# Segment sums of x moved from TensorE to GpSimd beside a VectorE-heavy scan stage

## The chip, the cores and the metric

One core of a Trainium2 chip (the jobs ran on different chips, each with runs of the kernel before beside it). The metric is device time in microseconds (us) of one execution. Engine names in profile lines: PE is TensorE (PEld its weight load), DVE is VectorE, ACT is ScalarE, POOL is GpSimd, SP is SyncE, whose queue issues most DMAs. SBUF and PSUM are the memories that the kernel's tiles lie in; the matmuls here write PSUM tiles (psP, psU, psR). A profile's span is about 1.7 us shorter than the time of the same execution (1262.2 and 1263.91 for the changed kernel). Times in the text count from the start of the profile's span.

## The reference, cut to what matters

Two independent branches, concatenated: a diagonal state space model (A) and a segment-recurrent attention with 8 memory slots (B).

```python
# A: per step t   h = Lam_bar * h + B_bar @ x[t];  y = 2 Re(C h) + x * D       (2048 steps, 1024 states)
# B: per segment of 32 tokens: h = [mem, xs]; q, k, v = h Wq, h Wk, h Wv
#    p = softmax(mask(q k^T * scale)); o = (p v) Wo; mem = o[:, :8]; out = o[:, 8:]
```

B's recurrence through `mem` is serial. The kernel avoids it by a guess: it estimates each segment's new memory from the mean of the segment's inputs (`xbar`), runs all segments at once, and at the end compares the guess with what came out. If the guess is off by more than a tolerance, a slow serial branch computes everything again. The change is about how the 64 segment sums behind `xbar` are formed.

## The kernel before

The stage that matters lasts from about 36 to 340 us. It interleaves two streams: 32 scan blocks of A (`stage1`, called block 0 to 31 below) and the value projection of B (`v_x`, four PSUM tiles each). One scan block, cut:

```python
for i in range(2):                       # TensorE: 16 matmuls into psU (2 buffers)
    for c in range(KC):
        PE.matmul(u[:, i, :], bt[:, i, c, :], xT[:, c, cols], ...)
V.tensor_tensor(pr, u (broadcast), tables, mult)        # a_pr: one input PSUM, one SBUF
V.tensor_tensor(w, w, pr[:, :, 1, :], add)              # both inputs SBUF
for j in range(2):
    V.tensor_tensor_scan(w[:, j], rr, w[:, j], carry)   # two scans, SBUF
    S.activation(g[:, j], w[:, j], Copy)                # a_g: ScalarE
# GpSimd: five tiny instructions (a_tt, a_nx) make the carry of the next block
V.tensor_tensor(n, g (broadcast), r3, mult)             # a_n: SBUF, SBUF
V.tensor_tensor(h, n[:, :, 0], n[:, :, 1], add)         # a_h: SBUF, SBUF
SP.dma_start(hs[tb][:, pc], h)
```

The segment sums, cut. `ind` is a 128 x 4 indicator of the four segments in a tile of 128 tokens:

```python
p = k.ps("R")
for t in range(16):                          # two tiles a block, blocks 3 to 10, before stage1
    for c in range(8):
        PE.matmul(p[:, o:o + 4], xr[:, c * 128:(c + 1) * 128], ind, start=True, stop=True)
    load(t + 4); yield
# VectorE: xbar = p / 40, plus mem0 in segment 0
```

The next reader of `xbar` (the matmuls called `og`) comes at 170 us.

## Time and profile before

| | before |
|---|---|
| time, median | 1247.91 us (1247.30 to 1248.12, 4 runs) |
| span of the profile | 1246.5 us |
| PE waits between 36 and 172 us | none |
| VectorE busy between 36 and 172 us | 116.55 of 136 us |

The page of the kernel before: the span, busy time of each engine, and the chain of work that ended last by engine.

```profile
span 1246.5 us, 20192 instructions
PE 1238.4 (99%) x8342; PEld 662.2 (53%) x8342; DVE 668.1 (54%) x1246; ACT 263.4 (21%) x631; POOL 276.5 (22%) x412
...
PE 97%; DMA 2%; ACT 1%; issue 0%; POOL 0%; DVE 0%; SPq 0%; ACTq 0%
```

The view by stretches, before. Columns: stretch, its length, then busy us and instruction count of PE, PEld, DVE, ACT and POOL, the granted TensorE clock, DMA share and GB/s.

```profile
36.00:172.00 136.00, 136.00 (x773) 63.87 (x772) 116.55 (x106) 55.75 (x99) 31.67 (x50) 1.00 0.62 168
```

PE is never idle here (136.00 of 136 us) and its granted clock is 1.00, so each microsecond taken from it should be gained. VectorE is at 86%.

One group of the sums on PE, before, in the timeline: start, length, engine, line, operation, output from input, shapes, count.

```profile
67.27 0.54 PE L64 MATMUL psR<-ind,b_xr 128*128 128x4 bf16 x16
67.67 0.59 PE L64 MATMUL psU<-a_xT,a_bt 128*128 128x512 bf16 x2
```

The 16 matmuls delay the next group by 0.40 us, 25 ns each. Four columns are only about a hundredth of a 512-column matmul, which takes 216 ns here (the 16 of one half into psU: 3.45 us), yet each of the small ones costs 25 ns, over a tenth of it. Eight such groups are 3.2 us of the critical path.

VectorE in block 5, before. The bracket at a line's end is the idle time before it and what ended it.

```profile
92.84 2.29 DVE L267 TENSOR_TENSOR a_pr<-psU,a_tabf 128x2048 f32<-128x2048 f32 x1 [1.18 <-PE psU L64]
95.17 1.23 DVE L270 TENSOR_TENSOR a_pr<-a_pr 128x1024 f32<-128x1024 f32 x1
96.50 2.46 DVE L275 TENSOR_TENSOR_SCAN a_pr<-a_rr,a_nx,a_pr 128x512 f32<-128x512 f32 x2
99.66 1.23 DVE L286 TENSOR_TENSOR a_n<-a_g,a_tabh 128x2048 bf16<-128x2048 bf16 x1 [0.69 <-ACT a_g L276]
100.92 0.69 DVE L287 TENSOR_TENSOR a_h<-a_n 128x1024 bf16<-128x1024 bf16 x1
103.60 2.29 DVE L267 TENSOR_TENSOR a_pr<-psU,a_tabf 128x2048 f32<-128x2048 f32 x1 [1.99 <-PE psU L64]
```

After `a_h` VectorE waits 1.99 us for PE: here it keeps up. In the blocks that also compute tables it does not, and idles less.

### The profile page before, as it was taken

What the parts mean: (1) busy time and instruction counts of PE and PEld (TensorE: products, weight loads), DVE (VectorE), ACT (ScalarE), POOL (GpSimd) and SP (SyncE); (2) the same over time, 40 slices, a digit from 0 to 9 for tenths busy, and PEclk for the clock granted to TensorE, in tenths of its full rate; (3) what the DMA queues carried; (4) which work ended last, traced back from release to release, by engine and by line L of the source; (5) the groups of instructions that cost most, each with busy time, mean ns of one, the idle gap of its engine ahead of it and who ended that gap; (6) DMA issues with size and microseconds to landing.
All of it is one profiled execution on the core that took longest, in us unless ns stands there. A gap on an engine that the chain in (4) does not pass through costs nothing.

```text
span 1246.5 us, 20192 instructions
## 1 busy us (share of the span) xinstructions
PE 1238.4 (99%) x8342; PEld 662.2 (53%) x8342; DVE 668.1 (54%) x1246; ACT 263.4 (21%) x631; POOL 276.5 (22%) x412
## 2 busy tenths in 40 slices
PE   9999999999999999999999999999999999999998
PEld 4444444444455555656666656555665554446444
DVE  4688899998711124666666666666666641001000
ACT  5344444443310000211111111111211110000000
POOL 4111331212322321322222222222222220000000
PEclk9999999999999999999999999999999999999999
DMA  9975444554898734665454544545473279407000
GB/s 236 267 205 150 130 131 128 144 156 108 240 322 248 250 116 94 182 176 122 96 144 108 144 108 113 138 91 133 97 155 95 60 222 225 107 18 153 17 17 27
DMA packets 316023, 176.83 MB, mean 142 GB/s; under 512 B 138651, under 2 KB 301327, under 8 KB 315927
## 3 DMA queue, kind: packets, MB, share of 16 engines
q1 hardware_dynamic: 293830, 147.95, 48.4%
q10 hardware_dynamic: 21072, 24.38, 5.8%
q0 software_dynamic: 1024, 3.17, 0.7%
q8 instruction: 66, 1.08, 0.4%
q14 instruction: 31, 0.25, 0.1%
HBM read 89.14 MB, written 53.17 MB: 114 GB/s over the span
## 4 chain that ended last, share of the span: by engine, by line
PE 97%; DMA 2%; ACT 1%; issue 0%; POOL 0%; DVE 0%; SPq 0%; ACTq 0%
PE psP L64 81%; PE psU L64 9%; PE psS L64 3%; PE psO L64 2%; PE psR L64 2%; DMA wo<-in_B_Wo_dram 1%; DMA b_vx<-b_vst 1%; DMA b_xr<-in_B_x_dram 0%; ACT b_vst L89 0%; ACT L187 0%; ACT b_xe L89 0%; POOL b_m L643 0%; ACT a_fr L236 0%; ACT a_k L233 0%; ACT a_k L229 0%
## 5 line engine op out<-in xcount | busy, mean ns | idle before, releaser
L64 PE MATMUL psP<-b_xe,b_wq 128*128 128x480 bf16 (+1 forms) x1280 | 247.7, 343 | 0.0
L64 PE MATMUL psP<-b_xe,b_wk 128*128 128x480 bf16 (+1 forms) x1280 | 247.7, 343 | 0.0
L64 PE MATMUL psP<-b_wv,b_xe 128*128 128x512 bf16 (+2 forms) x1048 | 224.6, 372 | 0.3 <-ACT b_xe L89 0.2
L643 POOL TENSOR_TENSOR b_m<-b_e,maskB 99x396 bf16<-99x396 bf16 x160 | 139.6, 872 | 334.8 <-ACT b_e L640 334.8
L640 ACT ACTIVATE b_e<-psS 99x396 bf16<-99x396 f32 x176 | 88.2, 501 | 532.8 <-PE psS L64 528.5
L64 PEld LDWEIGHTS <-b_wk 128*128 128x128 bf16 x1280 | 119.4, 98 | 94.2
L64 PEld LDWEIGHTS <-b_xe 128*128 128x128 bf16 x1056 | 101.9, 98 | 119.4 <-issue 0.6
L64 PEld LDWEIGHTS <-b_wq 128*128 128x128 bf16 x1280 | 118.7, 98 | 87.7
L91 DVE CAST b_k<-psP 128x480 bf16<-128x480 f32 (+1 forms) x192 | 98.2, 533 | 100.9 <-PE psP L64 100.9
L91 DVE CAST b_q<-psP 128x480 bf16<-128x480 f32 (+1 forms) x192 | 98.2, 533 | 93.1 <-PE psP L64 91.5
L64 PEld LDWEIGHTS <-b_ol 128*128 128x128 bf16 x864 | 84.3, 98 | 94.4
L64 PE MATMUL psU<-a_xT,a_bt 128*128 128x512 bf16 x512 | 114.9, 379 | 0.0
L64 PE MATMUL psP<-t,a_hl 128*128 128x512 bf16 x512 | 113.1, 379 | 0.0
L91 DVE CAST b_ost<-psP 128x512 bf16<-128x512 f32 (+1 forms) x17 | 11.5, 676 | 183.4 <-PE psP L64 183.4
L64 PE MATMUL psP<-wo,b_ol 128*128 128x512 bf16 (+1 forms) x448 | 92.5, 364 | 0.0
L64 PE MATMUL psP<-t,b_ol 128*128 128x512 bf16 x416 | 92.2, 379 | 0.0
L280 POOL TENSOR_SCALAR a_tt<-a_pr,a_tabf 128x1 f32<-128x1 f32 x48 | 34.1, 710 | 243.5 <-DVE a_pr L275 243.5
L660 DVE TENSOR_TENSOR b_ob<-psO,b_accR 99x384 bf16<-99x384 f32 x160 | 85.9, 553 | 2.5 <-DVE b_accR L659 0.3
L89 ACT ACTIVATE b_vst<-psP 128x512 bf16<-128x512 f32 x126 | 72.1, 589 | 71.4 <-PE psP L64 60.3
L267 DVE TENSOR_TENSOR a_pr<-psU,a_tabf 128x2048 f32<-128x2048 f32 x32 | 73.0, 2283 | 14.8 <-PE psU L64 14.7
L64 PEld LDWEIGHTS <-a_bt 128*128 128x128 bf16 x512 | 49.2, 98 | 57.6
L64 PEld LDWEIGHTS <-a_hl 128*128 128x128 bf16 x512 | 49.0, 98 | 56.7
(199 smaller groups left out, 964.2 us busy)
## 6 DMA issues: line engine op xcount, KB each, us to landing
b_v<-b_vx SPq DMA_DIRECT2D x16, 1122.0 KB
b_wv<-in_B_Wv_dram SPq DMA_DIRECT2D x16, 1024.0 KB
b_on<-b_ob SPq DMA_DIRECT2D x15, 960.0 KB
b_vx<-b_vst ACTq DMA_DIRECT2D x24, 544.0 KB
a_hs<-a_h SPq DMA_DIRECT2D x32, 256.0 KB
b_wog<-in_B_Wo_dram SPq DMA_DIRECT2D x4, 2048.0 KB
b_wq<-in_B_Wq_dram SPq DMA_DIRECT2D x16, 512.0 KB
b_wk<-in_B_Wk_dram SPq DMA_DIRECT2D x16, 512.0 KB
```

Of the source, the lines that this page charges most:

```text
L64: r = f(*a, **kw)
L89: self.S.activation(out, in_, ACT.Copy)
L91: self.V.tensor_copy(out, in_)
L267: V.tensor_tensor(pr[:], u[:].unsqueeze(1).to_broadcast([128, 2, 2, TB]), view(t3, [[TB + 1, 2], [TB + 1, 2], [1, TB]]), ALU.mult)
L280: G.tensor_scalar(tt[:, j:j + 1], w[:, j, TB - 1:TB], t3[:, 1, TB:TB + 1], None, ALU.mult)
L640: k.S.activation(e[:], s[0:GW], ACT.Exp, scale=float(E) ** -0.5, accum_out=self.accE[0:GW, i:i + 1])
L643: k.G.tensor_tensor(m[0:GW, 0:4 * GW].rearrange("p (a b q) -> p a b q", a=2, b=2), e[:], mask[0:GW, :, :].unsqueeze(2).to_broadcast([GW, 2 ...
L660: V.tensor_tensor(self.ob[:, b0:b0 + n, :], o[0:GW, 0:n, 0:E], r.unsqueeze(2).to_broadcast([GW, n, E]), ALU.mult)
```

## The change

It takes the 128 small matmuls off TensorE. Rows of x are loaded so that partition p holds tokens 16p to 16p+15. GpSimd adds the 16 rows in float32, two rows a scan block, placed behind the block's carry so that the carry isn't delayed. This leaves half-segment sums, split into a high and a low bfloat16 part; 16 matmuls with a 128 x 64 indicator join the halves.

```diff
-    k.ind = c.tile([128, 4], BF16, name="ind")
-    ... four memsets
+    k.ind = c.tile([128, NSEG], BF16, name="ind")
+    ... two affine_selects: 1 where partition // 2 == segment
 def sum_x:
-        for t in range(TT):
-            for c in range(KC):
-                k.PE.matmul(p[:, o:o + 4], xr[:, c * 128:(c + 1) * 128], k.ind[:], start=True, stop=True)
-            load(t + 4)
-            yield
+        for j in range(1, 16):
+            a = xrs.pop(0)[:] if j == 1 else acc
+            G("tensor_tensor", acc, a, xrs.pop(j)[:], ALU.add)      # pinned in program order
+            load(j + 3)
+            if j == 1:
+                load(4)
+            if j % 2 == 0:
+                yield
+        G("tensor_copy", hl[:, 0, :], acc)
+        yield
+        G("tensor_tensor", hl[:, 1, :], acc, hl[:, 0, :], ALU.subtract)
         yield
+        for c in range(KC):
+            for i in range(2):
+                k.PE.matmul(p[:, c * NSEG:(c + 1) * NSEG], hl[:, i, c * 128:(c + 1) * 128], k.ind[:], start=(i == 0), stop=(i == 1))
 main loop:
-                if n >= 3:
-                    for _ in range(2):
-                        next(sx, None)
                 a.stage1(pc, q)
+                if n >= 2:
+                    next(sx, None)
```

The adds fall in blocks 2 to 9, the copy in 9, the subtract in 10, the join after the matmuls of block 11.

More of the change, by code (lines that the diff above doesn't have):

```diff
@@ L106, in consts @@
     k.S.activation(k.hpe[:], k.hpb[:], ACT.Exp)
-    k.ind = c.tile([128, 4], BF16, name="ind")
-    G.memset(k.ind[:], 0.0)
-    for j in range(4):
-        G.memset(k.ind[32 * j:32 * j + 32, j:j + 1], 1.0)
+    k.ind = c.tile([128, NSEG], BF16, name="ind")
+    G.memset(k.ind[:], 1.0)
+    for base, m in ((0, 1), (1, -1)):
+        G.affine_select(out=k.ind[:], in_=k.ind[:], compare_op=ALU.is_ge, fill=0.0, base=base,
+                        pattern=[[-2 * m, NSEG]], channel_multiplier=m)
 def masks(k):
@@ L377, in fill @@
         z = tmp.tile([32, 4 * EW], BF16, name="b_xr", bufs=4)
-        k.V.memset(z[:], 0.0)
+        k.tc.keep_in_program_order(k.V.memset(z[:], 0.0))
         for hb in range(HB):
@@ L410, in turn_x0, with sum_x, G, load @@
         k.copy("vs"[i % 2], self.xe[:, :, 128 * i:128 * i + 128], pt)
-    def sum_x(self, tmp):
+    def sum_x(self, tmp, ct):
         k = self.k
+        def G(op, *a):
+            k.tc.keep_in_program_order(getattr(k.G, op)(*a))
+        acc, hl = ct[:, 0, 0:2, :].rearrange("p c d -> p (c d)").bitcast(FP32), ct[:, 0, 2:4, :]
+        rows = self.x[0].rearrange("(p j) d -> p j d", j=16)
         xrs = {}
-        def load(t):
-            if t < TT:
-                xrs[t] = tmp.tile([128, D], BF16, name="b_xr", bufs=4)
-                k.SP.dma_start(xrs[t][:], self.x[0][t * 128:(t + 1) * 128, :])
-        for t in range(4):
-            load(t)
+        def load(j):
+            if j < 16:
+                xrs[j] = tmp.tile([128, D], BF16, name="b_xr", bufs=4)
+                k.SP.dma_start(xrs[j][:], rows[:, j, :])
+        for j in range(4):
+            load(j)
+        yield
[8 more added lines that the diff above has]
+        G("tensor_copy", hl[:, 0, :], acc)
+        yield
+        G("tensor_tensor", hl[:, 1, :], acc, hl[:, 0, :], ALU.subtract)
         yield
         p = k.ps("R")
-        for t in range(TT):
-            xr = xrs.pop(t)
-            for c in range(KC):
-                o = c * NSEG + 4 * t
-                k.PE.matmul(p[:, o:o + 4], xr[:, c * 128:(c + 1) * 128], k.ind[:], start=True, stop=True)
-            load(t + 4)
-            yield
+        for c in range(KC):
+            for i in range(2):
+                k.PE.matmul(p[:, c * NSEG:(c + 1) * NSEG], hl[:, i, c * 128:(c + 1) * 128], k.ind[:], start=(i == 0), stop=(i == 1))
         pv = p[:].rearrange("p (c s) -> p c s", c=KC)
@@ L1019, in kernel_main @@
             loads = [[(b, 2)], [(a, 1), (a, 2)], [(b, 3), (a, 3)]]
-            sx = b.sum_x(p1)
+            sx = b.sum_x(p1, a.CT)
             tabs = {0: a.tabs}
```

## The prediction

> **What bounds it now.** TensorE. The page gives PE 99% busy of a 1246.5 us span at full clock, and the chain of waits is 97% PE; the list of waits between 30 and 330 us shows no PE wait at all. So a PE microsecond taken away is gained, and a PE wait put in is lost. VectorE is second in the stage touched: by stretches it is busy 31.95 of 35 us (101 to 136) and 32.6 of 36 (136 to 172).
>
> **Removed.** 128 matmuls psR<-ind,b_xr of 4 columns. The timeline of PE shows 8 groups of 16, each delaying the next group by 0.40 us (67.27 to 67.67): 3.2 us, all on the chain.
>
> **Added on PE.** 16 matmuls with 64 columns. The og matmuls of that shape take 0.93 us for 32 (170.62 to 171.55), so about 0.47 us. Net PE gain: 2.7 us, 0.2%.
>
> **Added on GpSimd.** 15 adds, a copy and a subtract of 128x1024. The same shape (a_xd) takes 2.12 us, so about 36 us between 68 and 150 us, on an engine 20 to 28% busy there. It fits, but it is not free:
>
> 1. VectorE and GpSimd. [...] an a_nx pair normally takes 0.53 us, but 3.56 us at 163.57, while VectorE runs two-input instructions back to back. So each add waits for, or blocks, the adds, scans and a_n/a_h products. The multiply that reads PSUM (a_pr, 2.29 us) should leave room for one add per block. I expect 4 to 10 us of VectorE delay by the tenth scan block. VectorE may lag 8 to 13 us before psU holds PE up, so this alone should cost PE nothing.
>
> 2. The join. In program order, which PE keeps, the 16 matmuls stand after stage1 of block 11. With the old groups gone PE gets there at about 146.7 us. They need the subtract, which is behind the carry of block 10; that carry ends at 147.8 us before. VectorE can be 2 to 3 us earlier (PE feeds it sooner, the xbar operations move back), but the contention makes it later. Subtract done at 148 to 156 us: a new PE wait of 1 to 9 us, which nothing gives back. This is the main doubt; the next reader of xbar is only at 170 us.
>
> 3. The SP queue, in order, now waits for adds before reloading row buffers. The load of b_wv for head block 2 (issued at 69.8 us, needed at 81) slips to about 74: perhaps 0 to 2 us of PE wait. One row is also loaded twice, which costs nothing by itself.
>
> **Sum.** -2.7 us, plus about 4.5 us of waits in 2 and 3: 1250 us, range 1244.8 (no wait) to 1257. Faster by over 2%: 1%; within 2%: 97%; slower by over 2%: 2%. If the subtract is in time, it is 1245.3.
>
> **What would show it.** Right: the ind matmuls fall from 128 to 16 and about 0.5 us; the waits of PE or its weight load show some us for GpSimd (subtract) near 147 us; adds of 2.1 us alone but up to 4 us against VectorE; everything after 330 us unchanged in length. Wrong: no wait there (then -2.7 us), or PE waits for psU (VectorE fell further behind than 8 us), or for b_wv.
>
> **What would make it wrong.** Adds much slower than 2.1 us in float32; the scheduler ordering VectorE differently, as at 109 us where a_pr of block 7 overtook a_n of block 6; [...] the scans starve and the lag passes 13 us (then 1260 or more).

## More of the kernel before

`v_x` does 8 matmuls into each psP tile (3 buffers), and ScalarE copies each tile out (`b_vst<-psP`). ScalarE's queue holds these copies and the `a_g` copies in one fixed order.

## The result

The changed kernel takes 1263.91 us (median of 4 runs, 1262.34 to 1263.99); before, 1247.91. The ratio is 1.0126, 95% interval 1.0109 to 1.0144. The forecast was 1250 with 1257 as the upper end: the direction was right, the loss was 16 us instead of 2.

The page after: span, busy times, chain by engine.

```profile
span 1262.2 us, 19918 instructions
PE 1238.3 (98%) x8159; PEld 661.3 (52%) x8230; DVE 689.3 (55%) x1246; ACT 263.6 (21%) x631; POOL 316.8 (25%) x427
...
PE 90%; DVE 7%; issue 1%; POOL 1%; DMA 1%; ACT 0%; SPq 0%; ACTq 0%; DVEq 0%
```

DVE does the same 1246 instructions, yet is busy 21.2 us longer, and 7% of the chain is now on it. POOL is 40 us longer; the forecast was about 36.

The view by stretches after, same columns.

```profile
36.00:172.00 136.00, 123.14 (x550) 54.92 (x560) 122.65 (x88) 50.15 (x88) 66.09 (x62) 0.96 0.60 162
```

The list of what PE waited for between 36 and 172 us, after: total us, times, longest. A third row, 0.2 us of issue before psU, is left out.

```profile
PE psP L64 <- ACT b_vst L89: 8.8, 4, 3.2
PE psR L64 <- POOL t L419: 3.2, 1, 3.2
```

PE is idle for 136 - 123.14 = 12.9 us, and its clock is 0.96 of full, another 0.04 x 136 = 5.4 us (an estimate; the clock has two places, so about 5). Less the 2.7 us of saved matmuls that is about 15.6 us, and the spans differ by 15.7. The `og` matmuls agree: the first group starts at 170.62 us before and 186.49 after, a later one at 308.10 and 323.97, both 15.9 us late. So all of the loss has arisen by the first `og`, whose lines are, before and after:

```profile
170.62 1.10 PE L64 MATMUL psR<-b_xbar,b_wv 128*128 128x64 bf16 x32
186.49 1.10 PE L64 MATMUL psR<-b_xbar,b_wv 128*128 128x64 bf16 x32
```

Where VectorE's 21 us come from: VectorE in block 5 after, to be held against the lines of before, and below it GpSimd at the same time.

```profile
99.69 1.23 DVE L271 TENSOR_TENSOR a_pr<-a_pr 128x1024 f32<-128x1024 f32 x1
101.02 2.46 DVE L276 TENSOR_TENSOR_SCAN a_pr<-a_rr,a_nx,a_pr 128x512 f32<-128x512 f32 x2
104.17 1.23 DVE L287 TENSOR_TENSOR a_n<-a_g,a_tabh 128x2048 bf16<-128x2048 bf16 x1 [0.70 <-ACT a_g L277]
105.43 2.65 DVE L288 TENSOR_TENSOR a_h<-a_n 128x1024 bf16<-128x1024 bf16 x1
108.00 2.28 DVE L268 TENSOR_TENSOR a_pr<-psU,a_tabf 128x2048 f32<-128x2048 f32 x1
```

```profile
104.41 1.05 POOL L283 TENSOR_TENSOR a_nx<-a_nx,a_tt 128x2 f32<-128x2 f32 x1
105.41 4.66 POOL L419 TENSOR_TENSOR t<-t,b_xr 128x1024 f32<-128x1024 f32 x2
```

`a_h` takes 2.65 us instead of 0.69. The last carry instruction (1.05 us from 104.41, against 0.20 at 115.03) lasts until about the end of `a_n` at 105.40; then the first add starts at 105.41, 0.02 us before `a_h`. That add ends at 107.5 (alone in the timeline it is 2.12 us long), and `a_h` 0.55 us later. The second add runs beside the next `a_pr`, which stays at 2.28 us. The idle time before `a_pr` is gone. So "behind the carry" is a costly place for one of the two adds and, in this block, a free place for the other.

The group of `a_h` after, 60 to 170 us (before, its mean is 683 ns), and VectorE's waits for psU from 60 to 200 us, first before, then after:

```profile
L288 DVE TENSOR_TENSOR a_h<-a_n 128x1024 bf16<-128x1024 bf16 x9 | 19.7, 2190 | 0.3
```

```profile
DVE a_pr L267 <- PE psU L64: 8.5, 6, 2.0
DVE a_pr L268 <- PE psU L64: 1.9, 2, 1.6
```

By the means of the groups, `a_h` makes up about 13.6 us of VectorE's growth. The rest is on the `a_pr` adds (about 3.9), the scans (3.3) and `a_n` (1.0), where an add ran at another moment: in block 3, which has no carry to wait for, one add ran beside the `a_pr` add (3.05 us instead of 1.23) and the next beside the two scans (4.13 instead of 2.46).

How a late VectorE reaches PE: ScalarE and PE after.

```profile
105.14 0.37 ACTq L509 DMA_DIRECT2D b_vx<-b_vst  x1
112.96 0.63 ACT L277 ACTIVATE a_g<-a_pr 128x512 bf16<-128x512 f32 x1 [7.85 <-DVE a_pr L276]
114.14 0.63 ACT L277 ACTIVATE a_g<-a_pr 128x512 bf16<-128x512 f32 x1 [0.55 <-DVE a_pr L276]
114.67 1.07 ACT L89 ACTIVATE b_vst<-psP 128x512 bf16<-128x512 f32 x2
```

```profile
107.21 5.34 PE L64 MATMUL psP<-b_wv,b_xe 128*128 128x512 bf16 x23
115.30 2.86 PE L64 MATMUL psP<-b_wv,b_xe 128*128 128x512 bf16 x8 [2.75 <-ACT b_vst L89]
```

ScalarE stands 7.85 us before `a_g`, for the scan. The copies that empty psP are behind it in its queue. PE fills its three psP tiles in 5.3 us and stops. A late VectorE thus stops PE through ScalarE's order and psP, not through psU, where the forecast looked for it.

Last, the clock. Short stretches after, same columns, around that wait:

```profile
107.00:115.00 8.00, 5.50 (x25) 2.44 (x25) 7.86 (x6) 1.49 (x3) 4.91 (x6) 1.00 0.76 193
115.00:117.00 2.00, 1.70 (x6) 0.68 (x6) 2.00 (x2) 1.36 (x4) 1.97 (x2) 0.77 0.00 0
117.00:119.00 2.00, 2.00 (x6) 0.73 (x5) 2.00 (x2) 2.00 (x5) 1.92 (x2) 0.50 0.00 0
119.00:121.00 2.00, 2.00 (x10) 0.83 (x8) 2.00 (x1) 0.85 (x2) 1.92 (x2) 0.88 0.00 0
```

After the wait the clock is 0.50 for a while, and 8 matmuls take 2.86 us instead of 1.89 (as at 127.56 us, after a wait of 1.78). It is so after the waits of 3.2 us at 129 and 160 us too: 0.53 and 0.50 in the stretches 133 to 135 and 164 to 166. A wait of 2.75 us was enough here, but in run 4 a wait of the same length was not followed by it (8 matmuls in 1.89 us); what decides it was not shown.

### The profile page after: what moved, and what is told of

Its sections match the earlier page's. It is cut to its first block, busy times and chain, and to the rows that moved or that the text cites. A ratio compares the mean times of both kernels' runs of the same rounds, so it can differ in the third digit from the quotient of the medians.

```text
span 1262.2 us, 19918 instructions
## 1 busy us (share of the span) xinstructions
PE 1238.3 (98%) x8159; PEld 661.3 (52%) x8230; DVE 689.3 (55%) x1246; ACT 263.6 (21%) x631; POOL 316.8 (25%) x427
## 3 DMA queue, kind: packets, MB, share of 16 engines
q0 software_dynamic: 1024, 3.17, 0.7%
## 4 chain that ended last, share of the span: by engine, by line
PE 90%; DVE 7%; issue 1%; POOL 1%; DMA 1%; ACT 0%; SPq 0%; ACTq 0%; DVEq 0%
PE psP L64 77%; PE psU L64 7%; PE psS L64 3%; PE psO L64 2%; DVE a_pr L276 2%; DVE a_pr L268 2%; PE psR L64 1%; DVE a_pr L271 1%; DVE a_h L288 1%; DVE a_n L287 1%; DMA b_wv<-in_B_Wv_dram 1%; ACT a_g L277 0%; POOL b_m L658 0%; POOL t L419 0%; SPq L64 0%
```

## The experiments

Theory: GpSimd's adds and VectorE's instructions with two SBUF inputs exclude each other (in block 5, `a_h` takes 2.65 us instead of 0.69 beside an add); VectorE falls behind, and with it ScalarE and PE. Rivals: the row loads or the join cause the loss; GpSimd is merely busy and the carry is late.

All outputs are right.

### 1. The adds alone: before_adds

```diff
 # kernel before, sums on TensorE kept
+        G("memset", xa, 1.0)                            # dead data
+        for j in range(1, 16):
+            G("tensor_tensor", acc, xa if j == 1 else acc, xa, ALU.add)
+            if j % 2 == 0: yield                        # two a block, after stage1, as in the change
+        ... tensor_copy, subtract
```

> The kernel before, whole, with the same 17 GpSimd instructions of 128x1024 added at the same places, on dead data, with no load, no join and no other change. Theory (the GpSimd adds and VectorE's two-input instructions exclude each other, so VectorE falls behind, ScalarE's queue with it, and TensorE waits for psP): VectorE busy 15 to 25 us more than before, TensorE waits of 6 to 15 us for psP between 80 and 180 us, time 1256 to 1266. Rival (the row loads behind the adds in the SP queue, or the join, make the loss): no change, 1248 to 1250.

1263.40 us against 1247.95, ratio 1.0121 (1.0104 to 1.0138). The loss is there with no load, no layout and no join changed. The line of busy times on its page:

```profile
PE 1240.2 (98%) x8270; PEld 663.7 (53%) x8342; DVE 689.0 (55%) x1246; ACT 262.9 (21%) x631; POOL 316.6 (25%) x430
```

Its list of PE's waits, 36 to 172 us:

```profile
PE psP L64 <- ACT b_vst L89: 10.6, 4, 4.9
```

### 2. The same occupancy without reading: before_writes

```diff
-            G("tensor_tensor", acc, xa if j == 1 else acc, xa, ALU.add)
+            G("iota", t, pattern=[[1, 2048]], ...)      # writes SBUF, reads nothing; 17 times
```

> As before_adds, but the 17 GpSimd instructions only write (an iota of 2048 integers, some 2 us each by the 0.56 us of one of 513) and read nothing of SBUF. Theory (the shared read is what excludes): VectorE busy within 3 us of before, no TensorE wait, 1247 to 1250. Rival (GpSimd being occupied delays the carry, whatever it does): as slow as before_adds.

1248.24 against 1247.95, ratio 1.0000 (0.9983 to 1.0017). The 17 instructions took 1.83 us each, 31 us in all (the 17 of run 1: 40), and VectorE's `a_h` kept its 683 ns. In the view of groups, those writes (count, busy us, mean ns), then `a_h`:

```profile
L449 POOL IOTA t<- 128x2048 int32 x17 | 31.2, 1834 | 0.7
...
L287 DVE TENSOR_TENSOR a_h<-a_n 128x1024 bf16<-128x1024 bf16 x11 | 7.5, 683 | 0.2
```

So neither GpSimd's occupancy nor a late carry makes the loss (1248.24 us); the instructions of run 1, which read SBUF, do: beside them the mean of `a_h` (60 to 170 us) was 1957 ns, beside the writes 683.

### 3. VectorE's time alone: before_dve

```diff
+            V.tensor_tensor(acc, xa if j == 1 else acc, xa, ALU.add)   # 17 on VectorE itself, pinned, after a_h
```

> The kernel before, with nothing new on GpSimd but one memset; instead VectorE itself does 17 adds of 128x1024 on dead data, two a block after a_h (1.2 us each by the a_pr add of the same size: 21 us, what VectorE got longer by in the changed kernel). Theory (the loss is VectorE's time and what hangs on it): 1258 to 1266, with TensorE waiting for psP behind ScalarE. Rival (the loss comes from GpSimd being late with the carry): 1248 to 1252.

1256.98 against 1247.38, ratio 1.0075 (1.0061 to 1.0090): below the range of the expectation. VectorE was busy 685.9 us, 17.8 more than before, though the 17 adds took 1.22 us each, 20.7 in all: records that follow each other closely overlap a little (two adds end at 106.88 us, the next `a_pr` starts at 106.80), and overlap counts once. That this is the whole difference was not checked. PE waited 6.4 us for psP behind ScalarE, and its clock in the stretch was 0.97. So loading VectorE alone, with GpSimd left alone, brings the same waits and more than half of the loss. The missing 3 us alone need not explain the rest of the gap to run 1; that the adds' place within a block matters as well is likely, but was not separated.

### 4. The join a block later: after_late_join

```diff
         yield
+        yield
         p = k.ps("R")
```

> The changed kernel with the 16 joining matmuls one scan block later (after stage 1 of block 12). Theory: the 3.2 us wait for the subtract goes, and the slow matmuls after it (about 1.3 us); the waits for psP stay: 1258 to 1261. If the join were the whole loss: 1246 to 1248.

1262.63 against 1247.95, ratio 1.0118. The wait for the subtract is gone, but the psP waits rose from 8.8 to 11.1 us; 1.3 us were gained (against the 1263.91 of the other job), not 3 to 6. The chain of the changed kernel suggests why: from 61 us until PE leaves the join at 163.7 over four fifths of it lie on VectorE, so a wait removed in one place can come back in another. The wait of 2.75 us in this run, without slow matmuls after it:

```profile
115.27 1.89 PE L64 MATMUL psP<-b_wv,b_xe 128*128 128x512 bf16 x8 [2.75 <-ACT b_vst L89]
```

### 5. One more buffer for psP: after_4psum

```diff
-                p = k.ps("P")[:]
+                p = k.ps("PPPR"[self.nv % 4])[:]       # psR's bank as the fourth
```

> The changed kernel with the psR bank, which is free until the join now, taken as a fourth buffer for the v projection. Theory (TensorE waits because ScalarE, in order behind a_g and so behind VectorE, frees psP late): each psP wait shrinks by up to one tile, 1.73 us, so 8.8 us of waits become 2 to 4 and the slow matmuls after them shrink too: 1254 to 1259. If psP were not the cause: unchanged, 1263 to 1265.

1277.68 against 1247.95, ratio 1.0235, slower than the change. Two things happened. Before the join the buffer gained a little: PE began the matmuls of block 11 at 153.45 us instead of 156.80. At the join all of it was lost again: PE waited 3.56 us for the psR bank and 2.72 for the subtract, and came out at 163.5 us, as in the changed kernel (163.7):

```profile
160.62 0.19 PE L64 MATMUL psR<-ind,t 128*128 128x64 bf16 x1 [3.56 <-ACT b_vst L89]
163.53 0.98 PE L64 MATMUL psR<-ind,t 128*128 128x64 bf16 x15 [2.72 <-POOL t L419]
```

All its waits for psP and psR up to 172 us were 13.9 us against 12.0. Later, `og`, which needs psR, waited for ScalarE's copies three times (2.5 to 3.8 us). That second part is a fault of the experiment, so its total time says nothing about the theory. The expectation (1254 to 1259) failed. That psP is where the wait shows and not what causes it is the likely reading, but this run does not show it.

### 6 and 7. One add a block, behind the carry or beside a_pr: before_one, before_one_gated

```diff
 # kernel before, nine adds on dead data, one in each of blocks 2 to 10
+            G("tensor_copy", g1, a.last_h[:, 1, TB - 1:TB])   # before_one_gated only: waits for a_h
+            G("tensor_tensor", acc, acc, xa, ALU.add)
```

> The kernel before with one add of 128x1024 on dead data behind the carry of each of the blocks 2 to 10 (9 instead of 17). Such an add starts when a_n ends and holds a_h back for some 2 us. Theory (what counts is where VectorE stands when the add starts): a_h from 0.69 to about 2.6 us in most blocks, VectorE busy 8 to 18 us more than before, and since VectorE has about 10 us of idle time there, 1249 to 1258. If half as many adds fit in the idle time for nothing: 1248.

> As before_one, but each add is preceded on GpSimd by a copy of one element of a_h, so that it starts only when a_h is done and runs beside a_pr, which reads PSUM. Theory: an add beside a_pr costs VectorE 0 to 0.3 us; VectorE busy within 4 us of before, no TensorE wait over 1 us, 1247.5 to 1249.5. If an add costs VectorE its length wherever it stands: as before_one.

Behind the carry: 1253.84 against 1247.78, ratio 1.0050 (1.0035 to 1.0066). Beside `a_pr`: 1248.81, ratio 1.0009 (0.9993 to 1.0024). The groups of `a_h`, first before_one, then before_one_gated:

```profile
L287 DVE TENSOR_TENSOR a_h<-a_n 128x1024 bf16<-128x1024 bf16 x11 | 17.0, 1549 | 0.2
```

```profile
L287 DVE TENSOR_TENSOR a_h<-a_n 128x1024 bf16<-128x1024 bf16 x11 | 7.5, 683 | 0.3
```

Nine adds of the same length cost 6 us in one place and about 1 us, near the noise, in the other. VectorE's total rose by 12.2 and 4.2 us (680.3 and 672.3). In these two runs, what an add costs is decided by what VectorE does when it starts.

### 8 and 9. Half of the columns on GpSimd: half, half2

Two adds of 512 columns take about as long as one `a_pr` (in half 2.39 us at 93.73, beside an `a_pr` of 2.28). TensorE keeps the left half.

```diff
+            gate()                                            # waits for a_h of the block
+            for t in (2 * n + 2, 2 * n + 3):
+                G("tensor_tensor", acc, acc, xrs[t][:, HF:D], ALU.add)
 # half: loads after the adds;  half2: loads before stage1
```

> The kernel before with only the right half of the columns summed on GpSimd (512 columns, two adds a block, started after a_h as in before_one_gated, so both should fit beside a_pr); the left half stays on TensorE as before. TensorE has 64 matmuls of 4 columns fewer and 8 of 64 more: 1.6 less 0.23, a gain of 1.4 us. Theory: VectorE busy within 4 us of before, no new TensorE wait, 1246 to 1247.5. If the adds cannot be hidden: 1249 or more.

> half with the row loads issued a block earlier in SP's queue (before the a_hs write of the block), as in the kernel before: half lost its time in TensorE's waits for the row tiles (7.6 us in the list of waits), not by VectorE, which was 5 us longer. Theory: no wait for b_xr, VectorE at most 6 us longer than before, 1246 to 1248.5.

half: 1256.80 against 1247.78, ratio 1.0075. It failed by its own load order: the loads stood behind the block's `a_hs` write in SP's queue, and the list of waits gives 7.6 us of PE's weight load for `b_xr`. half2 moved them ahead: 1246.27 against 1247.38, ratio 0.9990 (0.9977 to 1.0002). No PE wait is listed between 30 and 360 us. It is 1 us better by the medians, and the interval still contains 1.

### 10 to 12. The adds done by accumulating DMAs: acc_dma, acc_dma2, acc_dma3

A DMA can add into its destination: 14 of the 16 row DMAs of acc_dma do, all issued from GpSimd (0.95 us an issue), and its result was correct.

```diff
-            G("tensor_tensor", acc, a, xrs.pop(j)[:], ALU.add)
+            k.G.dma_start(accs[i], rows[:, j + i, :], accum_op=ALU.add)   # float32, two accumulators
 # then add the two, copy, subtract on GpSimd; join after block 12
 # acc_dma2: one add straight to bfloat16, no low part
 # acc_dma3: DMAs from block 0; the three instructions in blocks 8, 9, 10, each started after a_h
```

> The changed kernel with the 15 adds done by accumulating DMAs that GpSimd issues (two accumulators in float32, two rows a block from block 1), then one add, one copy and one subtract on GpSimd, join after stage 1 of block 12. Theory (only the adds' reading of SBUF on GpSimd made the loss): VectorE busy within 6 us of before, no psP wait over 1 us, and the TensorE gain of 2.7 us comes out: 1244.5 to 1247. If the join or the new layout cost time by themselves: above 1248. It is also open whether an accumulating DMA is fast enough; if GpSimd waits for one, the carry is late and the time goes above 1250.

> acc_dma without the high and low part: GpSimd does only one add, with the sum rounded to bfloat16, and TensorE joins with 8 matmuls; subtract and copy go, and the add stands three blocks ahead of the join. The rounding is coarser; if it were too coarse, the check at the end would send the program into its slow branch and the time would be far above 1300. Theory: the 0.6 us wait at the join goes, 8 matmuls less (0.23 us): TensorE's gain of 2.97 us, of which acc_dma showed about 1: 1244.5 to 1246.5.

> acc_dma with the accumulating DMAs one scan block earlier (from block 0) and the three GpSimd instructions spread over blocks 8, 9 and 10, each started after a_h as in before_one_gated; high and low part kept. acc_dma's profile shows what it lost of the 2.7 us: 0.6 us at the join, and VectorE held 2.0 us (an a_pr add) and 0.9 us (an a_h) by the add and the subtract. Theory: no wait at the join, VectorE at most 2 us longer than before, 1244.5 to 1246.5. If the rows' DMA traffic, at its peak in block 0, delays other loads: 1247 or more.

acc_dma: 1247.07 against 1247.78, ratio 0.9997 (0.9982 to 1.0012). Taking the 15 adds out of GpSimd's SBUF reads gives the 16 us back. (The row loads leave SP's queue too, but run 1 had the loss without touching them.) The time is just above the expected 1247. VectorE was 2.8 us longer than before.

acc_dma2 was correct but took 8326 us: without the low part the guess failed its check and the slow branch ran (133032 instructions in its profile; acc_dma has 19950). So the high and low split of the change is needed.

acc_dma3: 1245.13 against 1247.76, ratio 0.9982 (0.9968 to 0.9996), 2.6 us by the medians, about the whole PE gain. It beats the kernel before by 0.2%, the changed one by 1.5%. Its five times fall in two groups, 1245.1 (three) and 1247.0 (two), and the profile is of a run of 1247.01. The line of busy times on its page:

```profile
PE 1236.2 (99%) x8230; PEld 659.9 (53%) x8230; DVE 668.6 (54%) x1246; ACT 263.5 (21%) x631; POOL 295.7 (24%) x432
```

Its stretch, columns as above:

```profile
36.00:172.00 136.00, 134.43 (x666) 61.48 (x664) 116.71 (x105) 55.21 (x98) 49.22 (x73) 1.00 0.78 200
```

The one PE wait listed there:

```profile
PE psP L64 <- DMA b_wv<-in_B_Wv_dram: 1.6, 1, 1.6
```

VectorE is back at 668.6 us, before's value. The one loss is a weight tile that came late; the DMA share of the stretch is 0.78 instead of 0.62. That the faster three runs lack this wait fits the difference but was not profiled.

## Why the prediction was wrong, point by point

- **What bounds it, and what was removed: right.** PE was the limit; the ind matmuls cost 3.2 us and their successors about 0.5 us. acc_dma3 got 2.6 us.
- **The mechanism: right.** Adds on GpSimd and VectorE's two-input instructions excluded each other here (runs 1 and 2: `a_h` 1957 ns beside adds, 683 beside writes). Also right: one add a block fits beside `a_pr` (run 7: 1248.81 us against 1247.78).
- **"I expect 4 to 10 us of VectorE delay by the tenth scan block": mis-sized.** VectorE's busy time grew by 21.2 us. The prediction counted the free place beside `a_pr` but not where the other add starts: exactly between `a_n` and `a_h`, holding `a_h` for about 2 us in most blocks. `a_h` alone went from 683 ns to 2190 ns in the mean.
- **"VectorE may lag 8 to 13 us before psU holds PE up, so this alone should cost PE nothing": the step that failed.** psU never held PE. ScalarE's queue has psP's copies behind `a_g`, and psP gives only 5.3 us of work. It cost 8.8 us of waits plus the clock. And VectorE's added time, 21.2 us, is larger than its idle time before psU was: those waits fell from 8.5 to 1.9 us (60 to 200 us). So a further buffer would probably not have been enough; runs 4 and 5 fit this but do not prove it.
- **"a new PE wait of 1 to 9 us" at the join: right in size (3.2 us), wrong in weight.** It did not deserve to be the main doubt: run 4 removed it and gained 1.3 us.
- **b_wv late by "0 to 2 us": right**, 0.6 us of PE's weight load in the list of waits.
- **Not considered: the clock.** By the estimate above, about 5 us of the loss are matmuls at a lower clock after the longer waits (0.50 after 2.75 and 3.2 us).
- The prediction named a case in which "the lag passes 13 us (then 1260 or more)", outside its range. That number came, but not by that path: PE never waited for VectorE to free psU, and `a_h`, not the scans, took most of the delay.

## What to carry to other kernels

Before moving elementwise work to an idle GpSimd, write down what VectorE runs at the moment the work will start: where that had two SBUF inputs and the GpSimd instruction read SBUF, the two engines took turns here (`a_h` ended 0.55 us after the add, 2.65 us long instead of 0.69). To find how much lag an engine may have, follow every engine that waits on it, including in-order queues that hold unrelated work behind a dependent instruction, and ask about its rate, not only its buffers. Work that GpSimd only issues as accumulating DMAs, or starts behind an explicit dependence beside a PSUM-reading instruction, was nearly free here (acc_dma 1247.07 us against 1247.78, before_one_gated 1248.81 against 1247.78).

## What these runs leave open

- When GpSimd gets in between two-input instructions that VectorE issues back to back. Before the change a pair of tiny GpSimd instructions (128x1) that normally takes 0.53 us took 3.56 us at 163.57, over several VectorE instructions; yet in block 5 after, the add got in between `a_n` and `a_h`. No run separates the two cases. Two scans that take 2.46 us together took 4.13 us beside an add. That it takes two inputs was not shown: in half an `a_k` with one (128x513, at 127.07 us) took 1.26 us beside an add, and 0.43 in the changed kernel (at 85.14) with no add beside it.
- When the clock falls: a wait of 2.75 us was followed by a granted clock of 0.50 in the changed kernel, and one of the same length in after_late_join was not (8 matmuls in 1.89 us).
- What accumulating DMAs cost in general: here GpSimd spent 0.95 us on each issue of 128 x 1024 into float32 (mean of the 16 of acc_dma, two of which only write) and waited 13.2 us for earlier ones to land. In acc_dma3 two chains of eight ran beside the stage, and PE's only wait there was 1.6 us for the late weight tile.
